# A decode step on one core: the last Wo load in two parts, and three w_down loads cut into 112 partitions and small loads on few DMA engines

## The chip, the cores and the metric

One core of one Trainium2 chip. The metric is the time of one execution on the device in microseconds (us); lower is better. Runs of one kernel on one chip agree within about 0.4%.

## The reference, cut to what matters

```python
# x [2,1,640]; k_cache, v_cache [2,32,8192,192]; wq [640,6144]; wo [6144,640]
# w_gate, w_up [640,1536]; w_down [1536,640]; all bfloat16
q = layernorm(x) @ wq
scores, softmax and p @ v over the last 2048 keys of each of 32 heads
h  = x + o @ wo
h2 = h + (gelu(layernorm(h) @ w_gate) * (layernorm(h) @ w_up)) @ w_down
```

Two rows of activations read 122 MB of cache and weights once. So the kernel streams from device memory (HBM) into the on-chip memory (SBUF, 128 partitions), and the question is what stands between the last byte and the end.

## The kernel before: the parts that matter

All loads go through one ring buffer of 120 KB per partition, issued by SP (SyncE) in a fixed order: K and V of 16 groups, Wo in four pieces of 8 heads, then `w_gate`, `w_up`, and `w_down` in four chunks. A load starts when the piece of the ring that it overwrites has been used.

```python
def load_wo(J):                      # 8 heads: 128 partitions x 12 rows of 640
    load(("wo", J), 2 * 12 * D, A_wo[1536 * J:1536 * (J + 1), :].rearrange("(p kk) n -> p kk n", kk=12), ...)

def load_ffn():
    ...                              # w_gate, w_up: 15360 bytes on each of 128 partitions
    wd = B_w_down.rearrange("(r p j) n -> r p j n", p=128, j=3)
    for i, (f0, f1) in enumerate(WDC):              # four chunks, 3840 bytes on each partition
        load(("wd", i), 2 * (f1 - f0) * D, wd[i], ...)

def oproj(J):                        # h += o_J @ Wo_J
    ...
    for kk in range(12):
        for h in range(2):
            ins = e.matmul(m1[...], lhsT=ot[:, J % 2, kk, :], rhs=wo[:, kk, 320 * h:320 * (h + 1)], ...)
    pe(fn, R=wtoks + [("ot", J % 2), "xrow", "identb"], X=["m1"])
# ... cut ...
o_rows(3); oproj(2); o_columns(3); oproj(3)         # the tail begins here
h_columns(); layernorm(...)                          # -> hnT
ffn_in(sps, "s", "wg"); ...                          # gate, GELU
ffn_in(ops_, "o", "wu"); ...                         # up -> uT
for i, (f0, f1) in enumerate(WDC):                   # 12 matmuls for each w_down chunk
    pe(fn, R=["uT"] + wtoks, X=["m1"])
```

## Time and profile before

296.84 us median of 3 runs (296.07 to 297.12); the profiled execution has a span of 295.2 us.

| what | number | view |
|---|---|---|
| mean rate of the DMA engines | 415 GB/s | page, part 2 |
| DMA share of the chain that ended last | 69% | page, part 4 |
| last Wo piece landed | 276.94 us | chain |
| `uT` ready, w_down matmuls begin | 290.71, 290.76 us | chain |
| last w_up, last w_down landing | 286.15, 290.81 us | semaphore records of the trace |

The page's part 2 cuts the span into 40 slices. The first line is the busy share of the 16 DMA engines in tenths, the second what they moved.

```profile
DMA  7999999999999999999999999999999999999991
GB/s 277 433 441 437 431 426 422 426 422 433 435 419 442 426 440 426 426 420 426 428 430 426 435 436 425 430 435 426 426 425 436 432 430 425 430 420 424 426 388 73
```

The engines are busy nine tenths or more in every slice but the first and the last. Only the tail can change.

The chain that ended last, before, from its last DMA (start us, duration us, what; PE is TensorE, the matmul engine, DVE is VectorE; "issue" is time in which the engine waited for nothing that the profile shows):

```profile
247.30 29.64 DMA ring<-in_A_wo_dram
276.94 0.14 issue
277.07 1.80 PE m L622 x23
278.87 0.02 issue
278.89 0.49 DVE hrow L634
...
283.33 0.18 DVE hnT L326
283.52 0.04 issue
283.56 1.80 PE sps L691 x20
...
287.40 1.62 PE ops L691 x20
...
290.52 0.20 DVE uT L326
290.71 0.04 issue
290.76 1.80 PE m L737 x45
```

The chain leaves the DMA at the last Wo piece and from there is compute only: 1.80 us of Wo matmuls, layernorm, gate, up, w_down. No later load is on it.

Stretches of 2 us, before. The columns are the stretch and its length, busy us and instructions of PE, PEld (weight loads), DVE, ACT, POOL, then the granted TensorE clock, the DMA share and the rate. A packet is counted whole in the stretch in which it begins, so that a share can pass 1, and the share of a single stretch is good only to a tenth or so.

```profile
280.00:282.00 2.00, 1.26 (x16) 1.16 (x14) 0.60 (x4) 0.00 (x0) 0.00 (x0) 0.50 0.99 417
282.00:284.00 2.00, 1.03 (x10) 0.74 (x14) 0.23 (x2) 0.47 (x2) 0.00 (x0) 0.50 1.02 421
284.00:286.00 2.00, 1.33 (x21) 0.28 (x9) 0.56 (x1) 0.00 (x0) 0.00 (x0) 0.50 0.92 376
286.00:288.00 2.00, 2.00 (x23) 1.15 (x27) 0.82 (x5) 0.22 (x1) 0.00 (x0) 0.50 0.84 334
288.00:290.00 2.00, 1.34 (x18) 0.50 (x7) 1.13 (x4) 0.00 (x0) 0.00 (x0) 0.50 0.56 229
```

The rate sinks from 284 us on together with the share, and from 287.24 us on the first engines have finished (increments below). This is what a tail with engines out of step looks like.

The trace also holds each load's completion increments, 16 for a load of 128 partitions, as many as the page counts DMA engines. For the last w_down load, before (an extract of the semaphore records, us):

```
287.24 287.47 287.59 287.66 287.70 287.74 | 288.30 | 290.31 290.33 290.52 290.63 290.64 290.64 290.66 290.69 290.81
```

Six engines are done 3 us ahead of nine others. The packet records suggest why: the page lists 17 packets of the kind "instruction" on queue 8, 16 KB each (1.00 to 1.11 us in the packet records), and beside 16 of them (the last came after the w_down data) one engine's data packets break off for 1.0 to 1.1 us. With one such packet at 281.26 us, the eighth increment comes 1.52 us after the first when `w_gate` lands and 3.08 us when `w_up` does. That such packets are why nine engines end 3 us behind six is suggested by this, not shown.

### The profile page before, as it was taken

To read this page: it belongs to the slowest core of one execution; us is meant where nothing else is said; L and a number is where in the kernel's file an instruction comes from. 1 tells how busy PE (TensorE), PEld (TensorE's weight loads), DVE (VectorE), ACT (ScalarE), POOL (GpSimd) and SP (SyncE) were. 2 spreads that over 40 slices of the span, in tenths; PEclk is the share of its full clock that TensorE was granted. 3 is DMA by queue.
4 is the path that set the end of the run, shared out by engine and by line. 5 is a ranking of instruction groups with operands and counts; after the bars stand their busy time and mean duration, and the time that the engine had idled before them with its cause. 6 is when DMAs were issued, how large, how long until landed. Compare 5 with 4: busy or idle time off the path is not lost.

```text
span 295.2 us, 4895 instructions
## 1 busy us (share of the span) xinstructions
PE 194.2 (66%) x2141; PEld 152.0 (51%) x2141; DVE 130.2 (44%) x326; ACT 95.6 (32%) x119; POOL 2.7 (1%) x19
## 2 busy tenths in 40 slices
PE   2483467749486398749581686767697667685664
PEld 1461165719284385538450656564666464653332
DVE  5950555615256154435353352525266435254022
ACT  2150134614233063516251323434344334241000
POOL 3000000000000000000000000000000000000000
PEclk9995959997979689977998697979599979599555
DMA  7999999999999999999999999999999999999991
GB/s 277 433 441 437 431 426 422 426 422 433 435 419 442 426 440 426 426 420 426 428 430 426 435 436 425 430 435 426 426 425 436 432 430 425 430 420 424 426 388 73
DMA packets 6521, 122.61 MB, mean 415 GB/s; under 512 B 738, under 2 KB 740, under 8 KB 1252
## 3 DMA queue, kind: packets, MB, share of 16 engines
q1 hardware_dynamic: 6488, 122.29, 97.1%
q8 instruction: 17, 0.28, 0.4%
q14 instruction: 4, 0.03, 0.0%
q10 hardware_dynamic: 12, 0.00, 0.0%
HBM read 122.29 MB, written 0.00 MB: 414 GB/s over the span
## 4 chain that ended last, share of the span: by engine, by line
DMA 69%; PE 24%; DVE 4%; issue 1%; SPq 1%; ACT 0%; DVEq 0%; ACTq 0%
DMA ring<-in_A_k_cache_dram 50%; PE tps L474 17%; DMA ring<-in_A_wo_dram 10%; DMA ring<-in_A_wq_dram 9%; PE m L622 1%; PE ops L572 1%; DVE rq L326 1%; PE m L737 1%; PE sps L691 1%; PE m L605 1%; SPq L271 1%; PE ops L691 1%; PE tps L702 1%; DVE ktr L486 0%; PE m L641 0%
## 5 line engine op out<-in xcount | busy, mean ns | idle before, releaser
L474 PE MATMUL tps<-identf,ring 128*128 128x128 f32 x768 | 115.3, 319 | 50.0 <-DMA ring<-in_A_k_cache_dram 49.3
L474 PEld LDWEIGHTS tps<-identf,ring 128*128 128x128 f32 x768 | 107.2, 168 | 52.7 <-DMA ring<-in_A_k_cache_dram 50.6
L483 ACT ACTIVATE ktr<-tps 128x1024 bf16<-128x1024 bf16 x80 | 79.3, 1023 | 90.5 <-PE tps L474 90.0
L486 DVE COPY ktr<-tps 128x1024 bf16<-128x1024 bf16 x112 | 74.1, 688 | 77.5 <-PE tps L474 76.9
L547 ACT ACTIVATE eexp<-sm,nm 128x512 bf16<-128x512 f32 x16 | 11.5, 721 | 65.2 <-DVE nm L545 65.2
L572 PE MATMUL ops<-ring,ering 128*32 128x384 bf16 x512 | 23.7, 327 | 3.8 <-DMA ring<-in_A_v_cache_dram 3.7
L536 DVE CUSTOM_DVE_ANT_1 sm<-sps,mska 128x512 f32<-128x512 f32 x16 | 11.1, 691 | 34.2 <-PE sps L530 34.2
L530 PE MATMUL sps<-ktr,rq 128*16 128x512 bf16 x384 | 24.8, 390 | 0.3 <-DVE rq L326 0.3
L572 PEld LDWEIGHTS ops<-ring,ering 128*32 128x32 bf16 x512 | 12.4, 96 | 12.1 <-DMA ring<-in_A_v_cache_dram 5.7
L530 PEld LDWEIGHTS sps<-ktr,rq 128*16 128x16 bf16 x384 | 9.4, 88 | 10.7 <-issue 1.0
L543 PE MATMUL m<-mrhs,pm 128*128 128x16 bf16 x16 | 2.9, 183 | 18.1 <-DVE mrhs L322 18.1
L543 PEld LDWEIGHTS m<-mrhs,pm 128*128 128x128 bf16 x16 | 1.5, 96 | 25.8 <-DVE mrhs L322 25.8
L496 PE MATMUL tps<-ring,xnT 128*32 128x384 bf16 x80 | 5.1, 406 | 6.8 <-DMA ring<-in_A_wq_dram 6.8
L326 DVE TENSOR_TENSOR rq<-ops,mask 128x96 bf16<-128x96 f32 x16 | 2.7, 249 | 12.8 <-PE ops L514 12.8
L622 PE MATMUL m<-ring,ot 128*2 128x320 bf16 x96 | 5.3, 371 | 3.9 <-DMA ring<-in_A_wo_dram 3.9
L326 DVE TENSOR_TENSOR ering<-m,mask 128x256 bf16<-128x256 f32 x16 | 6.7, 419 | 2.5 <-PE m L556 2.4
L496 PEld LDWEIGHTS tps<-ring,xnT 128*32 128x32 bf16 x80 | 2.2, 114 | 9.5 <-DMA ring<-in_A_wq_dram 7.9
L378 ACT ACTIVATE lt<-m,eps_t 128x2 f32<-128x2 f32 x2 | 0.5, 262 | 20.2 <-PE m L376 20.2
L556 PE MATMUL m<-sel,eexp 128*128 128x64 bf16 x64 | 4.8, 202 | 1.2 <-ACT eexp L547 1.2
L556 PEld LDWEIGHTS m<-sel,eexp 128*128 128x128 bf16 x64 | 4.4, 106 | 1.6 <-DVE nm L545 1.3
L326 DVE TENSOR_TENSOR orow<-m,wm 128x1536 bf16<-128x1536 f32 x3 | 5.3, 1750 | 0.0
L622 PEld LDWEIGHTS m<-ring,ot 128*2 128x2 bf16 x96 | 2.3, 95 | 5.7 <-issue 2.5
(112 smaller groups left out, 80.7 us busy)
## 6 DMA issues: line engine op xcount, KB each, us to landing
ring<-in_A_k_cache_dram SPq DMA_DIRECT2D x16, 3072.0 KB, 27.5
ring<-in_A_v_cache_dram SPq DMA_DIRECT2D x16, 3072.0 KB, 29.8
ring<-in_A_wo_dram SPq DMA_DIRECT2D x4, 1920.0 KB, 30.9
ring<-in_A_wq_dram SPq DMA_DIRECT2D x2, 3072.0 KB, 21.0
ring<-in_B_w_gate_dram SPq DMA_DIRECT2D x1, 1920.0 KB, 33.9
ring<-in_B_w_up_dram SPq DMA_DIRECT2D x1, 1920.0 KB, 24.5
ring<-in_B_w_down_dram SPq DMA_DIRECT2D x4, 480.0 KB, 26.4
ring<-in_A_wq_dram SPq DMA_DIRECT2D x1, 1536.0 KB, 27.9
```

Of the source, the lines that this page charges most:

```text
L326: return lambda e: e.tensor_tensor(out=out, in0=a, in1=b, op=op)
L474: ins = e.transpose(tps[bi][:, 128 * u:128 * (u + 1)], kv[:, off:off + 128], identf[:, :])
L483: act(lambda e, dst=dst, bv=bv: e.activation(out=dst, in_=bv, func=ACT.Copy), W=[("kt", slot, n)], X=[("t", bi)])
L486: dve(lambda e, dst=dst, bv=bv: e.tensor_copy(dst, bv), W=[("kt", slot, n)], X=[("t", bi)])
L496: ins = e.matmul(tps[0][32 * r:32 * (r + 1), 0:384], lhsT=xnT[:, c, 32 * J:32 * (J + 1)], rhs=wq[:, c - c0, 1536 * J + 384 * r:1536 * J + ...
L530: ins = e.matmul(sps[32 * ch:32 * ch + 16, :], lhsT=rq[:, g, k, :], rhs=ktr[:, g % 2, k // 2, 1024 * ch + k % 2:1024 * (ch + 1):2], start= ...
L536: dve(lambda e: e.tensor_tensor_reduce(out=sm[:, :].rearrange("p (u x) -> p u x", u=4), in0=sps[:, :].rearrange("p (u x) -> p u x", u=4), ...
L547: act(lambda e: e.activation(out=eexp[:, :], in_=sm[:, :], func=ACT.Exp, bias=nm[:, 0:1], scale=1.0, accum_out=zr[:, g // 4 % 2, g % 4:g % ...
L556: ins = e.matmul(o, lhsT=eexp[:, 128 * u:128 * (u + 1)], rhs=sel64[:, :], start=True, stop=True)
L572: ins = e.matmul(ops_[32 * r:32 * (r + 1), 0:384], lhsT=ering[:, g % 4, t, :], rhs=vv[:, 384 * t:384 * (t + 1)], start=(g % 4 == 0 and t < 4),
L622: ins = e.matmul(m1[32 * r:32 * r + 2, 192:512], lhsT=ot[:, J % 2, kk, :], rhs=wo[:, kk, 320 * h:320 * (h + 1)], start=(kk == 1 or J > 0 a ...
L691: ins = e.matmul(bank[32 * r:32 * r + 2, 0:384], lhsT=hnT[:, c, :], rhs=wv[:, c, 384 * r:384 * (r + 1)], start=(c == 0), stop=(c == NC5 - ...
```

## The change

The intent has two halves. Wo of the last 8 heads is loaded in two parts, so that two thirds of its matmuls run while the last third is still in flight. And of three w_down chunks, 16 partitions are taken out of the load that all 16 engines share and given to loads of 3 rows, which run on three engines only, so that the engines that are behind have less to do.

```diff
+WDB = 3
+WDP = ((0, 112), (112, 115), (115, 118), (118, 121), (121, 124), (124, 127), (127, 128))
-        def load(key, nbytes, src, shape):
+        def load(key, nbytes, src, shape, parts=((0, 128),)):
...
-                P.op("sp", lambda e, v=v, src=src: e.dma_start(v, src), W=toks + [("sem", i % NSEM)], dma=f"d{i % NSEM}")
+                for n, (p0, p1) in enumerate(parts):
+                    P.op("sp", lambda e, v=v[p0:p1], src=src[p0:p1] if n or len(parts) > 1 else src: e.dma_start(v, src),
+                         W=(toks if n == 0 else [("part", key, n)]) + [("sem", (i + n) % NSEM)], dma=f"d{(i + n) % NSEM}")
...
+            for i, (k0, k1) in enumerate(wo_parts(J)):
+                load(("wo", J, i), 2 * (k1 - k0) * D, src[:, k0:k1, :], lambda v: v.rearrange("p (kk n) -> p kk n", n=D))
+        def wo_parts(J):
+            return ((0, 12),) if J < 3 else ((0, 8), (8, 12))
...
-                     lambda v: v.rearrange("p (s n) -> p s n", n=D))
+                     lambda v: v.rearrange("p (s n) -> p s n", n=D), WDP if i < WDB else ((0, 128),))
...
         def oproj(J):                                   # one pe() for each part, each waiting for its own load
+            for i, (k0, k1) in enumerate(wo_parts(J)):
```

More of the change, by code (lines that the diff above doesn't have):

```diff
@@ L254, in load @@
             off, i = pos[0], pos[1]
-            pos[0], pos[1] = off + nbytes, i + 1
-            queue.append((key, off, nbytes, src, shape, i))
+            pos[0], pos[1] = off + nbytes, i + len(parts)
+            queue.append((key, off, nbytes, src, shape, i, parts))
         def pump():
             while queue:
-                key, off, nbytes, src, shape, i = queue[0]
+                key, off, nbytes, src, shape, i, parts = queue[0]
                 old = [q for q in live if q[1] < off + nbytes and off < q[1] + q[2]]
@@ L269, in pump @@
                 toks = [("ring", x) for x in range(off // GRAN, (off + nbytes + GRAN - 1) // GRAN)]
-                where[key] = (v, toks)
-                P.op("sp", lambda e, v=v, src=src: e.dma_start(v, src), W=toks + [("sem", i % NSEM)],
-                     dma=f"d{i % NSEM}")
+                where[key] = (v, toks + [("part", key, n) for n in range(1, len(parts))])
+                for n, (p0, p1) in enumerate(parts):
+                    P.op("sp", lambda e, v=v[p0:p1], src=src[p0:p1] if n or len(parts) > 1 else src: e.dma_start(v, src),
+                         W=(toks if n == 0 else [("part", key, n)]) + [("sem", (i + n) % NSEM)], dma=f"d{(i + n) % NSEM}")
         def done(*keys):
@@ L293, in load_wo @@
         def load_wo(J):
-            load(("wo", J), 2 * 12 * D, A_wo[1536 * J:1536 * (J + 1), :].rearrange("(p kk) n -> p kk n", kk=12),
-                 lambda v: v.rearrange("p (kk n) -> p kk n", kk=12))
+            src = A_wo[1536 * J:1536 * (J + 1), :].rearrange("(p kk) n -> p kk n", kk=12)
+            for i, (k0, k1) in enumerate(wo_parts(J)):
+                load(("wo", J, i), 2 * (k1 - k0) * D, src[:, k0:k1, :], lambda v: v.rearrange("p (kk n) -> p kk n", n=D))
+        def wo_parts(J):
+            return ((0, 12),) if J < 3 else ((0, 8), (8, 12))
         def load_ffn():
@@ L611, in oproj, with fn @@
         def oproj(J):
-            wo, wtoks = where["wo", J]
-            def fn(e):
-                if J == 0:
-                    for h in range(2):
-                        e.matmul(m1[32 * h:32 * h + 2, 192:512], lhsT=identb[0:2, 0:2], rhs=xrow[0:2, 320 * h:320 * (h + 1)],
-                                 start=True, stop=False, tile_position=(0, 32 * h), skip_group_check=True)
-                for kk in range(12):
-                    for h in range(2):
-                        r = 2 * (kk % 2) + h
-                        ins = e.matmul(m1[32 * r:32 * r + 2, 192:512], lhsT=ot[:, J % 2, kk, :],
-                                       rhs=wo[:, kk, 320 * h:320 * (h + 1)], start=(kk == 1 or J > 0 and kk == 0) and J < 3,
-                                       stop=(J != 2 and kk >= 10), tile_position=(0, 32 * r), skip_group_check=True)
-                return ins
-            pe(fn, R=wtoks + [("ot", J % 2), "xrow", "identb"], X=["m1"])
-            done(("wo", J))
+            for i, (k0, k1) in enumerate(wo_parts(J)):
+                wo, wtoks = where["wo", J, i]
+                def fn(e, k0=k0, k1=k1, wo=wo):
+                    if J == 0:
+                        for h in range(2):
+                            e.matmul(m1[32 * h:32 * h + 2, 192:512], lhsT=identb[0:2, 0:2], rhs=xrow[0:2, 320 * h:320 * (h + 1)],
+                                     start=True, stop=False, tile_position=(0, 32 * h), skip_group_check=True)
+                    for kk in range(k0, k1):
+                        for h in range(2):
+                            r = 2 * (kk % 2) + h
+                            ins = e.matmul(m1[32 * r:32 * r + 2, 192:512], lhsT=ot[:, J % 2, kk, :],
+                                           rhs=wo[:, kk - k0, 320 * h:320 * (h + 1)], start=(kk == 1 or J > 0 and kk == 0) and J < 3,
+                                           stop=(J != 2 and kk >= 10), tile_position=(0, 32 * r), skip_group_check=True)
+                    return ins
+                pe(fn, R=wtoks + [("ot", J % 2), "xrow", "identb"], X=["m1"])
+                done(("wo", J, i))
             if J == 0:
```

## The prediction

The forecast's sum came to -0.7 us: 1.0 us from the Wo split, 0.85 of it left after the wait for w_up, less 0.1 to 0.2 us for waits, from 296.84 to 296.1 us. Terms are cut from the text below, where it is marked: which engines run the small loads, what these put on each, when those engines would be done, and the case that they are late ones, which the author put at 297 to 298 us ("a gap per small load would do the same" refers to it). That the small loads run on early engines was the assumption.

> **What bounds the kernel now.** The page shows the 16 DMA engines busy nine tenths or more in every slice but the first and last, at a mean of 415 GB/s, and 69% of the chain that ended last is DMA. None of those 122 MB goes away: the change touches only the tail. There the chain of waits sits on the last Wo load (heads 24-31) until 276.94 us, then runs on without a hole: 24 matmuls of L622 (1.80 us), layernorm, gate, up, GELU, `uT` at 290.70, 48 matmuls of w_down (L737, 1.80 us), cast, store, end at 295.2. PE could have begun that projection at 275.0 (timeline: `ot` ends at 274.99).
>
> The completion increments in the trace (16 per load, one per engine) show that the engines do not keep step. The last w_down load lands on six engines at 287.24-287.74, on one at 288.30, on nine at 290.31-290.81. An engine lost 1.0-1.1 us whenever a 16 KB instruction packet (DMA queue 8, 17 of them) cut into its stream. [...]
>
> **What the change does.**
> 1. Wo: 8 of 12 rows per partition come first. Two thirds of the 4.6 us between the last two Wo landings puts them at about 275.4. Their 16 matmuls (four groups of 0.267 us, timeline) run in the shadow of the rest; 8 remain after about 277.0. Saved on the chain: 1.0 us.
> 2. w_down: a row of 3840 B takes 0.151 us on an engine (packet records). In three chunks each engine gives up one of 8 rows: -0.45 us in all. The freed 16 rows go in loads of 3. [...] The late ones end at about 290.4.
> 3. 18 more w_down issues on SP at about 0.46 us: 8 us from 262 on, long before the data is due. 19 more waits on PE (51 ns each in the trace), six hidden ahead of the `uT` wait, the others partly behind queued matmuls: 0-0.3 us.
>
> **How much is on the path.** w_up lands at 286.15; its matmuls start at 287.17 and would be ready at 286.1, so they begin at about 286.3: 0.85 us of the 1.0 is left. The last w_down chunk is wanted at about 291.1 and is there. Less 0.1-0.2 us for waits: -0.7 us, a quarter of one per cent.
>
> **Prediction: 296.1 us, 80% range 295.3 to 297.2. Faster by over 2%: 1%; within 2%: 97%; slower by over 2%: 2%.**
>
> **What would show it.** L622's wait splits in two, the last part 8 matmuls; a new short wait of the up projection for w_up; `uT` at 289.8; w_down increments within about 1 us of one another, none after 290.5; no wait of PE for w_down.
>
> **What would make it wrong.** [...] A gap per small load would do the same. The early Wo part could land late if instruction fetches shift.

## The result, and the profile after

299.43 us median of 6 runs (299.06 to 299.62) against 296.85 us (296.07 to 297.18, 6 runs): ratio 1.009, 95% interval 1.0073 to 1.0107. It is slower by 2.6 us, under 1%, but clear of the noise and outside the predicted range. The profiled span is 297.5 us.

The end of the chain, after:

```profile
275.53 18.62 DMA ring<-in_B_w_down_dram
294.15 0.04 issue
294.19 0.60 PE m L743 x10
294.79 0.02 issue
294.81 0.33 DVE yrow L749
```

The chain now leaves the DMA at the last w_down chunk, 294.15 us, where before it left at Wo. Only that chunk's matmuls, the cast and the store follow.

PE's waits for DMA in the tail, after (engine and line, what it waited for: us in total, times, longest):

```profile
PE ops L697 <- DMA ring<-in_B_w_up_dram: 2.6, 1, 2.6
PE m L628 <- DMA ring<-in_A_wo_dram: 1.9, 3, 0.8
PE m L743 <- DMA ring<-in_B_w_down_dram: 0.5, 1, 0.5
```

Before, the only DMA wait of PE in the tail was Wo's:

```profile
PE m L622 <- DMA ring<-in_A_wo_dram: 3.9, 2, 2.3
```

The Wo half did its job (its longest wait is 0.8 instead of 2.3 us; the timeline has `hnT` begin at 281.87, 1.46 us earlier). But the up projection then stands 2.6 us for w_up, which landed at 288.48 instead of 286.15, although its load was not changed at all. The last w_down landing went from 290.81 to 294.15. Both count, though the chain shows only the second: without the wait for the last chunk the w_down matmuls would have ended at 292.06 + 1.80 = 293.86 us, against 292.56 before and 294.79 now (worked out from the chains and the timeline), so 1.3 us of the loss came by way of w_up and 0.9 through the last chunk.

The same stretches, after:

```profile
280.00:282.00 2.00, 0.59 (x2) 0.50 (x2) 0.63 (x5) 0.47 (x2) 0.00 (x0) 0.50 0.99 415
282.00:284.00 2.00, 1.77 (x20) 0.52 (x20) 0.13 (x2) 0.00 (x0) 0.00 (x0) 0.50 1.03 311
284.00:286.00 2.00, 1.41 (x11) 0.57 (x11) 1.04 (x5) 0.00 (x0) 0.00 (x0) 0.50 1.02 238
286.00:288.00 2.00, 0.00 (x0) 0.00 (x0) 0.83 (x4) 0.22 (x1) 0.00 (x0) 0.50 1.00 230
288.00:290.00 2.00, 1.48 (x20) 0.51 (x20) 0.00 (x0) 0.00 (x0) 0.00 (x0) 0.50 0.97 204
```

In 284 to 286 us the DMA share is 1.02 and the rate is 238 GB/s. The engines are busy all the time and move less than two thirds of what they moved before (376). They do not idle between small loads; each packet takes longer. The packet records agree: a w_down row takes 235 ns on average (151 before), and the rows of w_up that started in 284 to 286 us take 1001 ns (579 before), on late engines that have not come to w_down yet. The slowing begins when the first early engine starts the 112-partition load: w_down packets begin at 282.27, and the w_up rows that start at 282.31, 282.45 and 282.71 take 629, 676 and 1011 ns. The first completion increment of a 3-row load comes only at 285.47.

### The profile page after: what moved, and what is told of

Its sections match the earlier page's. It is cut to its first block, busy times and chain, and to the rows that moved or that the text cites. A ratio compares the mean times of both kernels' runs of the same rounds, so it can differ in the third digit from the quotient of the medians.

```text
span 297.5 us, 4923 instructions
## 1 busy us (share of the span) xinstructions
PE 197.7 (66%) x2141; PEld 152.1 (51%) x2141; DVE 130.6 (44%) x326; ACT 95.5 (32%) x119; POOL 2.7 (1%) x19
## 4 chain that ended last, share of the span: by engine, by line
DMA 69%; PE 20%; SPq 5%; DVE 3%; issue 1%; ACT 0%
DMA ring<-in_A_k_cache_dram 53%; PE tps L479 17%; DMA ring<-in_A_wq_dram 9%; DMA ring<-in_B_w_down_dram 6%; SPq L272 5%; PE ops L577 1%; DVE rq L331 1%; DVE ktr L491 1%; PE tps L501 1%; DVE ering L331 0%; PE m L628 0%; PE m L610 0%; PE ops L519 0%; ACT qrow L508 0%; PE m L591 0%
## 5 line engine op out<-in xcount | busy, mean ns | idle before, releaser
L577 PE MATMUL ops<-ring,ering 128*32 128x384 bf16 x512 | 24.9, 338 | 5.6 <-DMA ring<-in_A_v_cache_dram 5.5
L535 PE MATMUL sps<-ktr,rq 128*16 128x512 bf16 x384 | 26.0, 405 | 0.3 <-DVE rq L331 0.3
L501 PE MATMUL tps<-ring,xnT 128*32 128x384 bf16 x80 | 5.7, 444 | 7.3 <-DMA ring<-in_A_wq_dram 7.3
L628 PE MATMUL m<-ring,ot 128*2 128x320 bf16 x96 | 4.1, 298 | 1.9 <-DMA ring<-in_A_wo_dram 1.9
L610 PE MATMUL m<-selb,orow 128*128 128x2 bf16 x48 | 3.5, 200 | 2.2 <-DVE ering L331 1.6
```

Of the source, the lines that this page charges most:

```text
L501: ins = e.matmul(tps[0][32 * r:32 * (r + 1), 0:384], lhsT=xnT[:, c, 32 * J:32 * (J + 1)], rhs=wq[:, c - c0, 1536 * J + 384 * r:1536 * J + ...
L535: ins = e.matmul(sps[32 * ch:32 * ch + 16, :], lhsT=rq[:, g, k, :], rhs=ktr[:, g % 2, k // 2, 1024 * ch + k % 2:1024 * (ch + 1):2], start= ...
L577: ins = e.matmul(ops_[32 * r:32 * (r + 1), 0:384], lhsT=ering[:, g % 4, t, :], rhs=vv[:, 384 * t:384 * (t + 1)], start=(g % 4 == 0 and t < 4),
```

## The experiments

Theory A: the engines collide where they write, so that the partitions that a load writes decide what it costs. In the change a load of 112 partitions leaves 16 increments, so that each of 16 engines has seven rows instead of eight (an estimate, 112 over 16), and a 3-row load sends three engines (three increments each) to partitions 112 to 127. Theory B: small loads cost by themselves, or give three engines too much. Theory C: something before the engines, as the issue on SP or reads that clash in memory.

What the expectations below said of which engine writes which partitions, and so of which engines meet, no trace or run shows. The expected numbers stand as estimates. How many engines a load uses is shown for some sizes: in the trace after, loads of 1, 3, 112 and 128 rows left 1, 3, 16 and 16 increments. For the loads of 16 and 64 partitions below, 16 engines are the assumption, as it is that all one-row loads of `spare_single` go to one engine.

All results in one table. "Rate" is the last column of the 284 to 286 us stretch; "w_up rows" is the mean packet of w_up (15360 bytes) that began in that stretch; landings are the last increments.

| run | median us | ratio to before, 95% | rate GB/s | w_up rows ns | w_up, last w_down landed |
|---|---|---|---|---|---|
| before | 296.85 | | 376 | 579 | 286.15, 290.81 |
| after | 299.43 | 1.009 (1.0073 to 1.0107) | 238 | 1001 | 288.48, 294.15 |
| wo_only | 296.07 | 0.9971 (0.9957 to 0.9984) | 373 | 577 | 286.10, 290.80 |
| wd_only | 299.32 | 1.0077 (1.0064 to 1.0091) | 244 | 989 | 288.49, 293.81 |
| wd_112_16 | 299.44 | 1.0086 (1.0072 to 1.01) | 242 | 988 | 288.85, 294.66 |
| wd_halves | 299.92 | 1.0105 (1.009 to 1.0119) | 248 | 928 | 288.57, 295.39 |
| wd_columns | 296.08 | 0.9973 (0.9958 to 0.9988) | 368 | 576 | 286.18, 291.03 |
| spare_low | 296.32 | 0.9981 (0.9966 to 0.9996) | 384 | 577 | 286.27, 290.95 |
| spare_high | 300.06 | 1.0106 (1.0089 to 1.0123) | 236 | 876 | 287.59, 294.80 |
| spare_one | 298.16 | 1.0045 (1.003 to 1.006) | 348 | 597 | 286.28, 292.86 |
| spare_shift | 299.28 | 1.0085 (1.007 to 1.01) | 259 | 911 | 287.25, 293.99 |
| wd_stride8 | 300.74 | 1.0132 (1.0117 to 1.0147) | 246 | 955 | 288.48, 295.21 |
| spare_single | 298.42 | 1.0056 (1.0039 to 1.0074) | 367 | 611 | 287.04, 293.21 |

The experiments ran in three groups (`wo_only`, `wd_only`, `wd_112_16`, `wd_halves`; `spare_low`, `spare_high`, `spare_one`, `wd_columns`; the last three), the first on another chip than the other two, each beside "before" (297.08, 296.95 and 296.88 us). All diffs below are against the changed kernel, or against `wo_only` where that is said.

### The two halves apart: wo_only and wd_only

```diff
-WDB = 3
+WDB = 0                                                  # wo_only
```
```diff
-            return ((0, 12),) if J < 3 else ((0, 8), (8, 12))
+            return ((0, 12),)                            # wd_only
```

> Only the Wo split; w_down loaded as before. All theories: the Wo step kept its 1.0 us in the changed kernel too (the chain reached hnT 1.4 us earlier), so the loss is all in the w_down loads. Expect 295.9 us, 0.6 to 1.1 us under the kernel before; w_down packets back at 0.151 us, w_up landing at 286.2, last w_down landing at 290.8. If it is slower than before, the Wo split is to blame as well.

> Only the w_down change; Wo in one load. Every theory that puts the loss in the w_down loads expects the changed kernel's time, 299.4 us, as w_up and the last w_down chunk end the chain there and neither waits for Wo: w_up landing near 288.5, last w_down near 294.

Both as expected. The Wo half alone gives 296.07 us (5 runs, 295.99 to 296.09), 0.3% under the kernel before and, with `wd_columns`, the best of all kernels here. One thing limits this gain: the executions of the kernel before lie on two levels. Of all 29, 23 took 296.68 to 297.31 us, but six took 296.05 to 296.35, close to what `wo_only` always takes. The trace kept of "before" is of the upper level (297.04 us), none of the lower was kept, and what sets the level stays open. So the split is worth about 1 us against most executions and little against the best. The w_down half alone has the whole loss; in the changed kernel the Wo half's gain vanished, since it only made the up projection wait longer for w_up (2.6 us with the Wo split, 1.3 us in `wd_only`). The chain of `wo_only` from the last Wo landing:

```profile
276.92 0.04 issue
276.96 0.73 PE m L628 x6
277.69 0.02 issue
277.72 0.49 DVE hrow L640
...
286.21 1.73 PE ops L697 x20
...
289.45 0.19 DVE uT L331
```

The row sum starts 1.17 us earlier than before (277.72 against 278.89) and `uT` 1.07 us earlier (289.45 against 290.52): nearly all of the saving is carried through.

### Without 3-row loads: wd_112_16

```diff
-WDP = ((0, 112), (112, 115), (115, 118), (118, 121), (121, 124), (124, 127), (127, 128))
+WDP = ((0, 112), (112, 128))
```

> Wo split; each of three w_down chunks as 112 partitions and one load of 16 partitions, both on 16 engines: 7 + 1 rows per engine, no 3-row loads, no engine with more bytes. Theory A (engines collide at the partitions that they write[...]) expects it as slow as the changed kernel or slower, 298.5 to 301 us, with w_down packets of 0.2 us and more and w_up rows of 1 us beside them. Theory B (cost and imbalance of the 3-row loads) expects the time of the Wo split alone, 296 us, with packets of 0.151 us. Theory C (the late issue of 18 more loads on SP) expects 296 us too.

299.44 us. Without any 3-row load and with only three loads more on SP (and, if the 16 partitions are spread over 16 engines as assumed, without more bytes on any engine), the loss is all there. Theory B falls for this change, and so does the late issue on SP.

### 128 partitions in two ways: wd_halves and wd_columns

```diff
+WDP = ((0, 64), (64, 128))                               # wd_halves
```
```diff
+WDP = ((0, 2), (2, 3))                                   # wd_columns, with
-        v=v[p0:p1], src=src[p0:p1] if n or len(parts) > 1 else src
+        v=v[:, p0:p1] if len(parts) > 1 else v, src=src[:, p0:p1] if len(parts) > 1 else src
```

> Wo split; three w_down chunks each as partitions 0 to 63 and 64 to 127, 16 engines and 4 rows each: same bytes per engine, 3 more loads in all. Theory A expects [...] w_down packets of 0.3 us, rate near half, the last w_down landing at about 294 and 298 to 300 us. Theories B and C expect 296 us and packets of 0.151 us.

> Control for the halves: Wo split; three w_down chunks each as two loads of all 128 partitions, 2560 and 1280 bytes of every row. As many more loads as in the halves (3), more packets (+384). Theory A expects 296.1 us, packets at 25 bytes per ns, last w_down landing at 290.8 to 291.2. If splitting a chunk in two costs by itself, it shows here.

Both as theory A expected, though milder in the halves: w_down rows took 0.24 us on average, not 0.3, and the rate fell to two thirds, not to near half; the last chunk still came later than expected (295.39 us). Cut along partitions, 299.92 us; cut along columns into as many loads with more packets, 296.08 us, the time of `wo_only`. The stretch 284 to 286 us of `wd_halves`, then that of `wd_columns`:

```profile
284.00:286.00 2.00, 1.33 (x15) 0.57 (x11) 0.83 (x3) 0.00 (x0) 0.00 (x0) 0.50 0.98 248
```

```profile
284.00:286.00 2.00, 1.33 (x15) 0.56 (x11) 0.86 (x3) 0.00 (x0) 0.00 (x0) 0.50 0.94 368
```

Nearly the same share busy (0.98 and 0.94), two thirds of the rate (248 and 368 GB/s).

### The destination alone: spare_low, spare_high, spare_one, spare_shift

These four keep the whole 128-partition loads of `wo_only` and add the same 18 loads of 3 rows (the first left three increments, below), six behind each of three w_down chunks. Their data is read by nobody; at the end SP also waits for them. Only the partitions that they write differ: p, p+4 and p+8, which the expectations write as p+4i, and in `spare_one` three in a row. The diff is against `wo_only`.

```diff
+SPB = (0, 32)                # spare_low; (112, 80) in spare_high; (16, 48) in spare_shift
...
+                if key[0] == "wd" and key[1] < 3:
+                    for n in range(6):
+                        r, p0 = key[1], SPB[n // 4] + n % 4
+                        row = 384 * r + 3 * (110 + 3 * n)
+                        P.op("sp", lambda e, r=r, p0=p0, w=B_w_down[row:row + 9, :].rearrange("(q j) n -> q (j n)", j=3):
+                             e.dma_start(ktr[p0:p0 + 9:4, 0, r, 0:3 * D], w), ...)
```
`spare_one` writes `ktr[p0:p0 + 3, ...]` with p0 in 0, 32, 4, 36 instead of every fourth partition.

> The Wo-split kernel with 18 loads of 3 rows added, six behind each of the first three w_down chunks, whose data nobody reads (a dead part of ktr)[...]. [...] Theory A [...] expects packets of 0.151 us, the three engines 2.8 us later (ending near 290.7), nothing on the late engines, and 296.1 us, within 0.3 of the Wo split alone. Theory B (small loads cost by themselves) and theory C (reads of the same w_down rows clash in memory) expect slow packets, as in the changed kernel: 298 us or more.

> The same 18 loads, same engines and same source rows, but into partitions p+4i with p in 112 to 115 or 80 to 83[...]. Theory A expects both sides to slow: packets of 0.25 to 0.3 us [...], w_up 1 to 2 us late [...], the last w_down landing at 292.5 to 294 and 297.5 to 299 us. Theories B and C expect the same time as with the low partitions.

> The same 18 loads again, into three partitions in a row (p, p+1, p+2 with p in 0, 32, 4, 36)[...]. Theory A expects rows of 0.4 us and more [...], 18 of them, so that these three end 4 to 5 us later than with the spread partitions: last w_down landing at 294 to 296, 299.5 to 301.5 us, while w_up (the late engines) stays at 286.1. Theories B and C expect no difference from the spread partitions.

The stretches 284 to 286 and 286 to 288 us of `spare_low`:

```profile
284.00:286.00 2.00, 1.34 (x19) 0.57 (x11) 0.74 (x2) 0.00 (x0) 0.00 (x0) 0.50 0.94 384
286.00:288.00 2.00, 2.00 (x28) 0.52 (x20) 1.21 (x6) 0.22 (x1) 0.00 (x0) 0.50 0.91 363
```

and of `spare_high`:

```profile
284.00:286.00 2.00, 1.34 (x15) 0.57 (x11) 0.89 (x3) 0.00 (x0) 0.00 (x0) 0.50 0.93 236
286.00:288.00 2.00, 0.60 (x12) 0.20 (x12) 1.06 (x6) 0.22 (x1) 0.00 (x0) 0.50 1.00 265
```

The same loads of the same rows cost 0.25 us in one place and 4.0 us in the other (296.32 and 300.06 against the 296.07 of `wo_only`, which ran on another chip). In `spare_low` all 566 rows of 3840 bytes that began after 282 us took under 165 ns, so 18 small loads are nearly free, and their small size, their source and their issue are cleared. The three increments of the first of them came at 284.19, 284.23 and 284.79 us, right behind the early engines' own rows, while nine engines ended their rows of the chunk before it only at 287.03 us and later: the engines that such loads use are early ones, as assumed.

Two expectations missed in size. `spare_high` was slower than expected, because all late engines slowed and not only a few (w_up rows 876 ns on average, 577 in `spare_low`). `spare_one` cost less than expected (298.16 us, expected at least 299.5): the last w_down load lands at 292.86 us, 1.91 us later than in `spare_low`, but w_up rows hardly slow (597 ns on average). That opened a new question, which the next runs put: who slows? Theory A1: two engines that meet slow each other and nobody else ("sharing"). Theory A2: only writing into the other half hurts, partitions 64 to 127, where `spare_low` did not write. Theory A3: wherever engines meet, everybody slows.

### Low partitions in another place: spare_shift, wd_stride8

```diff
-WDP = ((0, 112), ..., (127, 128))
+WDP = tuple((j, 128, 8) for j in range(8))               # wd_stride8; v[slice(*pp)], src[slice(*pp)]
```

> The high-partition run slowed all late engines[...]. [...] Here the same 18 loads of 3 rows go to partitions p+4i with p in 16 to 19 or 48 to 51[...]. Theory A1 (sharing slows the sharers): some 3-row packets of 0.2 to 0.3 us, w_up rows on the late engines untouched at 0.577 us, 296.2 to 297.2 us. Theory A2 (only writing into the other half hurts): [...] 296.3 us, packets of 0.151 us. Theory A3 [...]: w_up rows of 0.8 to 1.1 us and 299 to 300 us.

> Wo split; each of three w_down chunks in eight loads of 16 partitions 8 apart (p, p+8, ..., p+120), one row on each of 16 engines[...]. Theories A1 and A3 expect packets of 0.25 to 0.3 us and 298 to 300 us, as in the halves. [...]

`spare_shift` differs from `spare_low` in one number: the partitions are 16 higher. It took 299.28 us against 296.32. The same two stretches:

```profile
284.00:286.00 2.00, 1.33 (x15) 0.57 (x11) 1.01 (x4) 0.00 (x0) 0.00 (x0) 0.50 1.02 259
286.00:288.00 2.00, 0.79 (x16) 0.35 (x16) 0.94 (x5) 0.22 (x1) 0.00 (x0) 0.50 0.98 277
```

So writing into the upper half is not needed (theory A2 falls), and w_up rows on late engines slow too, to 911 ns (A1 falls here); time and rows are those of A3. `wd_stride8` slows as well: the output is right, and it takes 300.74 us, a little over what was expected, the slowest of all. It does not bear on A2: each of its loads writes into both halves, and from which half an engine came was not shown.

### One row in each small load: spare_single

```diff
-                             e.dma_start(ktr[p0:p0 + 9:4, 0, r, 0:3 * D], w), ...)      # spare_high
+                             e.dma_start(ktr[p0:p0 + 1, 0, r, 0:3 * D], w), ...)        # with 3 source rows of 640
```

The expectation holds two cases: first that one other engine is slowed, then that many are.

> As the high-partition run, but each of the 18 loads is one row, all on one engine: 18 rows instead of 54[...]. [...] w_up rows stay at 0.577 us on all but one engine and the time is 296.3 to 297.2 us. [...] most w_up rows after 284 us take 0.65 us or more and the time is 297 to 298.5 us.

298.42 us is in the second range, but the rows are those of the first. W_up rows stayed at 575 to 602 ns, except two that followed each other on one engine, 818 and 1140 ns; that engine landed w_up 0.9 us after all others. The increments of the last w_down load (an extract of the semaphore records) show who was slow:

```
287.49 287.59 287.66 287.69 287.88 288.18 290.43 290.51 290.60 290.69 290.75 290.76 290.80 290.85 | 292.40 | 293.21
```

Fourteen engines end as in `wo_only` (290.80 us there at the latest, 290.85 here); two pay, at 292.40 and 293.21 us, one of them presumably with the 18 rows more to move (2.7 us by themselves, an estimate from 0.151 us each). So the one-row loads slow two engines, against A3 as it was worded; no view names the two. The 3-row loads of `spare_shift` and `spare_high` slow everybody (w_up rows 911 and 876 ns on average): rank by rank, the 16 increments of the last w_down load come 1.5 to 3.1 us later in `spare_shift` than in `spare_low`.

## Why the prediction was wrong

- **Wo (item 1): right.** 1.0 us predicted; `uT` came 1.07 us earlier in `wo_only`, and the median fell by 1.0 us (the two levels of the kernel before, above, bound what that is worth). The expected loss of 0.15 us to a wait for w_up did not come: w_up landed at 286.10 and PE was busy until 286.21.
- **Which engines the small loads use: right.** They were early ones (increments from 284.19 us in `spare_low`), three of them: after, the second w_down chunk lands on four engines at 286.23 to 286.90 us, on three at 288.45 to 289.04 and on nine at 291.23 to 291.82.
- **"A row of 3840 B takes 0.151 us on an engine": the step that failed.** The prediction took this duration from loads of 128 partitions, and carried it to loads of 112 and of 3. After the change a row took 0.235 us on average, and rows of w_up in flight beside them 1.0 us instead of 0.58. So "the late ones end at about 290.4" became 290.24 to 294.15 over all engines, and w_up, taken as fixed at 286.15, landed at 288.48. `spare_low` against `spare_shift` (296.32 and 299.28 us) shows that the destination does it, and `wd_112_16` (299.44) that the loss needs no 3-row load. PE then waited 2.6 us for w_up and 0.5 us for the last w_down chunk, where the prediction had a short wait and none.
- **"What would make it wrong" named three cases** (the small loads on late engines; a gap per small load; a late early part of Wo). None occurred: the small loads ran on early engines, the packets got longer with no gap between them (share 1.02), and the early part of Wo landed at 275.33 us, where 275.4 was expected.
- **SP issue and PE waits (item 3): harmless, as said,** though the issue was mis-sized: 22 w_down issues took 15.3 us, not the 10 that 0.46 us each makes. They ended at 276.6 us, well ahead of 282.3, when the first of the data moved. The w_down matmuls began 0.06 us after `uT` in spite of six more semaphores to wait for.
- **Even the intent could hardly have worked.** Moving a row to another engine does not move it to another partition: the rows that the change hands over still go to partitions 112 to 127, and in `spare_high` 3-row loads to partitions from 112 and 80 on cost 4.0 us. That is argued from the runs, not measured in one of its own.

Left open: why the 3-row loads of `spare_shift` and `spare_high` slow the late engines at large (w_up rows of 911 and 876 ns on average) when the one-row loads of `spare_single` slow only two engines, and what sets the partitions of `spare_low` apart. No view names an engine or the partitions that it writes; that engines meet where they write is the reading of these runs, not shown by a view.

## What to carry to other kernels

Read share and rate together: engines that are busy all the time at less than two thirds of the rate (after, 1.02 and 238 GB/s instead of 376) were, in these runs, slowed by which partitions were written (`spare_low` 296.32, `spare_shift` 299.28 us), and not by when they were fed. While other loads ran, three loads of 128 partitions cut along their columns cost nothing (`wd_columns` 296.08, `wo_only` 296.07 us) and cut along their partitions over 3 us (`wd_halves` 299.92); of the four placements of the small loads only one was nearly free (`spare_low`, partitions from 0 and 32 on, 0.25 us). And before carrying a packet's duration over to a load of another shape, measure it there: a w_down row took 151 ns in loads of 128 partitions and 235 after the change. The best change here is the Wo half alone: 296.07 us. There the last w_down chunk lands at 290.80 us and PE, which takes 0.45 us per chunk from 289.68, asks for it at about 291.0 (worked out from these two numbers), so a further gain has to shorten both.
